# Weight sums by accumulating transfers in DRAM, and one first-layer quadruple on both pairs of K blocks

## The chip, the cores and the metric

The kernel runs on one core of one Trainium2 chip. The metric is device time of one execution in microseconds. The core's engines are TensorE (PE in the profile, with its weight loads as PEld), VectorE (DVE), ScalarE (ACT), GpSimd (POOL) and SyncE (SP, which here only issues DMAs). A difference of about 0.2% is what a measurement of this kernel can tell from none.

## The reference, cut to what matters

```python
q, k, v = x @ wqkv                     # x: 2048 x 640, 32 heads of 20
idx = pos[:, None] - 2 * arange(8)     # each position sees 8 keys, 2 apart
attn = softmax(where(idx >= 0, (q . k[idx]) * scale, -1e9))
a = (attn . v[idx]) @ wo               # 640 x 640
h = x @ w1 + b1                        # 640 x 1728
b = (h * tanh(softplus(h))) @ w2       # Mish, 1728 x 640
g = sigmoid((x * gate_w).sum(-1))
out = g * a + (1 - g) * b              # all in float32
```

## The kernel before, in words

**Precision.** Every float32 operand of a matmul is split into two parts of the fast type fp32r: ACT copies the tile (high part, L466), then POOL or DVE subtracts the high part from the tile (low part, L469). A block product is then three matmuls (high x high, high x low, low x high; `mm3`, L534 to L536), on 128 x 128 weights and 512 or 496 columns.

**Seven products for eight.** Most of the work is written as 2 x 2 blocks and done by the Strassen-Winograd scheme: seven block products in place of eight, on sums of the operands. For activations these sums are the forms t1 to t4; for weights they are s1 to s4. A sum is made once and then split like any other operand.

**Stages.** Tokens are cut into four blocks of 512 (tb), two in each half P. In half 0 and then half 1: projection units u.0 to u.7 (a unit is 8 heads of one half, eight slots of 15 matmuls; units 2 and 3 are done by a pair scheme, `Two`), and quadruples q.P.0 to q.P.5 of the first layer (hidden blocks q and 7 + q, both token blocks of the half, five K blocks: 20 block products if done plainly). Attention of the eight units runs on DVE beside it, from unit to unit, far into the next stage. Then the second layer (`mlp2`, L1414) for all tokens, as products a, b, c, e, g, d, f over seven K steps, and last the output projection `wo_part` (L1580) for each half.

**The quadruple.** Class `Quad` (L1142) applies the seven products to both pairs of K blocks (0, 1 with 2, 3) and does the fifth K block plainly: 18 block products. Class `Single` (L1823) applies them to one pair only: 19. `Plain` takes 20. Its steps are `first`, `second`, `m1` to `m4`, `l1`, `l2`; between them ACT copies a bank of PSUM into the next as its seed (`seed`, L1171). `KIND` (L256) names the class for each quadruple of half 1; half 0 always uses `Quad`. `Quad` needs the forms of x for K pairs 0 and 1, `Single` those of pair 0 only (`x_forms`, L1056).

**Weight sums of the first layer.** `pieces` (L1077) loads a quadruple's weight blocks and makes s1 to s4 by additions on POOL or DVE (`combined`, L1040 to L1046, seen as L1044), in half 0 on 256 columns at a time and in half 1, for `Single`, on 128 columns (four additions for each quadruple). Half 1 makes them again from the weights.

**Weight sums of the second layer and of wo.** `sums_of` (L1251) is called nine times (the word `sum` in the order): it loads two blocks of weights, makes three sums and one more of a narrow part on POOL or DVE (L1266, L1279), a negated copy on ACT (L1285), and stores five pieces in DRAM. Later `load_pair` or `load_two` load and split them. `load_minus` and `load_minus_two` load weights with their sign turned, by ACT and DVE.

**What sets the order.** `Plan` (L69) is a list scheduler that runs while the kernel is built: every operation is a task with an engine, a modelled duration, a rank, the tasks it waits for and the buffers it takes from rings (24 pairs, 8 raw tiles, 8 hidden tiles). `ORDER` (L260) is a text that lists the steps of the first stages; a task's place in it breaks ties of rank. A task marked ANY goes to POOL, or to DVE when it is due within 8 us of TensorE's need (`NEAR`). `BANKS` (L259) says which of two groups of three PSUM banks a step uses. DMAs on SP are issued in the order of the plan; transfers that add to their destination (`accum_op`) are issued by POOL, in order with its other work (L955, L1554).

Of the kernel before, what the change touches and what calls it, by code (L numbers as in the profile page):

```python
# [8 lines left out]
F32 = mybir.dt.float32  # L9
# [268 lines left out]
def kernel(ctx: ExitStack, tc: tile.TileContext, x, wq, wo, w1, b1, w2, out):  # L278
# [125 lines left out]
    s_d = [dram.tile([128, 1280], F32, name=f"s{kc}") for kc in range(KH)]  # L404
# [382 lines left out]
    class Two:  # L787
# [16 lines left out]

        def load_first(self):
            n, w = self.n, self.w
            for i in self.pairs:
                (ra, da), (rb, db), (rc, dc), (rd, dd) = [self.raw(self.hq + h, k, n) for h, k in ((0, i), (1, i), (1, 2 + i), (0, 2 + i))]
# [322 lines left out]
    def last_pieces(P):  # L1131
# [7 lines left out]
        if P:  # L1139
            W1["second"] = ws  # L1140
# [864 lines left out]
```

## Time and profile before

| what | value |
|---|---|
| three timed runs | 613.5, 613.86, 613.88 us (median 613.86) |
| the profiled execution's own time | 614.11 us |
| its span, first to last instruction | 612.3 us |
| granted TensorE clock | 1.000 |
| DMA | 147.01 MB, mean 240 GB/s |

Durations in the prediction come from the profiled execution, whose time stands 1.81 us above its span and 0.25 us above the median of the timed runs. In a row of instructions in order of time the first number is the start in microseconds, the second the duration; then come engine, line, operation, the tile written and the tile read with their shapes, how many instructions are merged in the row, and in brackets the idle time before it and what ended that. A row of a group gives its count, total busy time, mean duration in nanoseconds, and the engine's idle time before it. A row of a stretch gives the busy time of PE, PEld, DVE, ACT and POOL, the granted clock, the DMA engines' busy share and GB/s. A queue's row gives its packets, MB and the time its packets took, as a share of 16 engines' span. A row of transfers gives their count, size and the median time from issue to landing.

### The profile page before, as it was taken

The numbers are of one execution on the slowest core, as the hardware profiler recorded it, in microseconds if no ns is written. First come the engines' busy times: TensorE is split into PE (matmuls) and PEld (weight loads), VectorE is DVE, ScalarE is ACT, GpSimd is POOL, SyncE is SP. The second block draws the span as 40 slices with busy tenths as digits, with TensorE's granted clock in tenths as the row PEclk, the third lists the DMA queues.
The fourth block names the chain that finished last, engine by engine and source line by source line (L and its number), as shares of the span: only waits on it lengthen the run. The fifth ranks groups of instructions, "written<-read, shape, count | busy, mean of one in ns | idle before, by whom it ended". The sixth has DMA issues, their size and how long they took to land.

```text
span 612.3 us, 9208 instructions
## 1 busy us (share of the span) xinstructions
PE 608.3 (99%) x2710; PEld 505.7 (83%) x2710; DVE 578.6 (94%) x517; ACT 387.4 (63%) x887; POOL 354.9 (58%) x334
## 2 busy tenths in 40 slices
PE   9999999999999999999999999999999999999997
PEld 7888888888888888888888888888888888888886
DVE  8799998999999999999999999999999999989956
ACT  7678567766897575666656775784966653736520
POOL 1666799978788915464579566686359864001000
PEclk9999999999999999999999999999999999999999
DMA  9764796749788688876888799989798874979913
GB/s 323 227 206 139 239 280 194 269 150 313 278 288 262 188 235 221 257 235 185 225 243 277 226 318 284 346 236 267 232 329 239 231 226 140 279 251 303 279 65 120
DMA packets 101346, 147.01 MB, mean 240 GB/s; under 512 B 11616, under 2 KB 54624, under 8 KB 101072
## 3 DMA queue, kind: packets, MB, share of 16 engines
q1 hardware_dynamic: 97936, 140.66, 71.1%
q0 software_dynamic: 3072, 5.51, 6.4%
q8 instruction: 21, 0.34, 0.3%
q14 instruction: 29, 0.24, 0.1%
q10 hardware_dynamic: 288, 0.26, 0.1%
HBM read 92.38 MB, written 53.03 MB: 237 GB/s over the span
## 4 chain that ended last, share of the span: by engine, by line
PE 97%; ACT 1%; DVE 1%; issue 0%; POOL 0%
PE qb L534 16%; PE qb L535 16%; PE qb L536 16%; PE sb L535 16%; PE sb L536 16%; PE sb L534 16%; PE qb L698 1%; DVE raw L1044 1%; ACT pair L466 1%; PE sb L442 1%; PE sb L540 0%; PE qb L541 0%; PE sb L541 0%; PE qb L540 0%; POOL raw L1044 0%
## 5 line engine op out<-in xcount | busy, mean ns | idle before, releaser
L469 POOL TENSOR_TENSOR pair<-raw,pair 128x512 fp32r<-128x512 f32 (+3 forms) x136 | 169.5, 1269 | 69.0 <-ACT pair L466 46.9
L466 ACT ACTIVATE pair<-raw 128x512 fp32r<-128x512 f32 (+3 forms) x235 | 137.1, 611 | 53.9 <-DMA raw<-actt 12.6
L536 PE MATMUL sb<-pair,pair 128*128 128x512 f32 (+1 forms) x396 | 153.0, 386 | 0.0
L534 PE MATMUL sb<-pair,pair 128*128 128x512 f32 (+1 forms) x396 | 153.0, 386 | 0.0
L535 PE MATMUL sb<-pair,pair 128*128 128x512 f32 (+1 forms) x396 | 153.0, 386 | 0.0
L534 PE MATMUL qb<-pair,pair 128*128 128x512 f32 (+1 forms) x377 | 145.6, 386 | 0.0
L535 PE MATMUL qb<-pair,pair 128*128 128x512 f32 (+1 forms) x377 | 145.5, 386 | 0.0
L536 PE MATMUL qb<-pair,pair 128*128 128x512 f32 (+1 forms) x377 | 145.4, 386 | 0.0
L591 DVE TENSOR_TENSOR pr<-kvq,qg 128x2560 f32<-128x2560 f32 x32 | 89.8, 2807 | 3.3 <-ACT qg L597 2.3
L637 DVE TENSOR_TENSOR pr<-kvq,pg 128x2560 f32<-128x2560 f32 x32 | 90.2, 2820 | 1.0
L594 DVE TENSOR_REDUCE lg<-pr 128x128 f32<-128x2560 f32 x32 | 90.2, 2818 | 0.7
L641 DVE TENSOR_REDUCE kvq<-pr 128x320 f32<-128x2560 f32 x32 | 90.0, 2814 | 0.4
L534 PEld LDWEIGHTS sb<-pair,pair 128*128 128x128 f32 x396 | 74.3, 188 | 14.9
L535 PEld LDWEIGHTS sb<-pair,pair 128*128 128x128 f32 x396 | 74.3, 188 | 14.8
L536 PEld LDWEIGHTS sb<-pair,pair 128*128 128x128 f32 x396 | 74.3, 188 | 14.7
L534 PEld LDWEIGHTS qb<-pair,pair 128*128 128x128 f32 x377 | 70.8, 188 | 14.4 <-ACT qb L1171 0.5
L536 PEld LDWEIGHTS qb<-pair,pair 128*128 128x128 f32 x377 | 70.8, 188 | 13.8
L535 PEld LDWEIGHTS qb<-pair,pair 128*128 128x128 f32 x377 | 70.8, 188 | 13.7
L469 DVE TENSOR_TENSOR pair<-raw,pair 128x512 fp32r<-128x512 f32 (+3 forms) x99 | 68.6, 714 | 3.7 <-ACT pair L466 3.5
L1044 POOL TENSOR_TENSOR hb<-hb,hb 128x512 f32<-128x512 f32 x42 | 55.0, 1327 | 11.7 <-ACT hb L1177 4.8
L1044 POOL TENSOR_TENSOR raw<-raw,raw 128x128 f32<-128x128 f32 (+3 forms) x49 | 40.5, 840 | 12.9 <-DMA raw<-in_wq 2.9
L469 POOL TENSOR_TENSOR pair<-hb,pair 128x512 fp32r<-128x512 f32 (+2 forms) x29 | 34.9, 1210 | 15.7 <-DMA act<-hb 5.8
(173 smaller groups left out, 755.1 us busy)
## 6 DMA issues: line engine op xcount, KB each, us to landing
actt<-hb SPq DMA_DIRECT2D x52, 256.0 KB, 4.0
raw<-in_w SPq DMA_DIRECT2D x40, 256.0 KB, 4.0
act<-hb SPq DMA_DIRECT2D x38, 256.0 KB, 4.2
raw<-actt SPq DMA_DIRECT2D x37, 256.0 KB, 2.6
raw<-in_wq SPq DMA_DIRECT2D x36, 248.0 KB, 4.0
raw<-act SPq DMA_DIRECT2D x29, 256.0 KB, 4.4
raw<-in_x SPq DMA_DIRECT2D x27, 256.0 KB, 4.0
o<-ot SPq DMA_DIRECT2D x64, 80.0 KB, 3.2
```

Source lines behind the costliest of these rows:

```text
L442: nc.tensor.matmul(warm_banks[i % 3].t[:, :n], ones[:, :128], ones[:, :n], start=i < WARM, stop=True, skip_group_check=True)
L466: a = add("ACT", act_ns(n), lambda: A.activation(hi(), raw(), AF.Copy), after, rank=rank, take=take, hold=hold)
L469: return (V if e == "DVE" else G).tensor_tensor(lo(), raw(), hi().bitcast(F32), op=OP.subtract)
L534: nc.tensor.matmul(ps, ah, bh, start=first, stop=False, skip_group_check=more)
L535: nc.tensor.matmul(ps, ah, bl, start=False, stop=False, skip_group_check=more)
L536: nc.tensor.matmul(ps, al, bh, start=False, stop=last, skip_group_check=more)
L591: return V.tensor_tensor(pr, window(kv, s0, 0), qg[:, :, None, :].to_broadcast([128, 2, W, QF]), op=OP.mult)
L594: V.tensor_reduce(lg_w[:, s0:s0 + 2], pr.rearrange("p s w (h d) -> p s w h d", d=DH), op=OP.add, axis=AX.X)
L637: V.tensor_tensor(pairs.rearrange("p s k i (h d) -> p s k i h d", d=DH), vw, pg[:, s0:s0 + 2].rearrange("p s (k i) h -> p s k i h", i=2)[: ...
L641: V.tensor_reduce(q[:, s0:s0 + 2], pairs.rearrange("p s k i f -> p s f k i"), op=OP.add, axis=AX.XY)
L698: nc.tensor.matmul(ps.t[:, :n], X[0, kc].t[:, a, i * 128:(i + 1) * 128], WQ[0, kc].t[:, b, :n], start=a == b and kc == 0, stop=False)
L1044: return (V if e == "DVE" else G).tensor_tensor(t.t[:, i:i + n], a.t[:, j:j + n], b.t[:, k:k + n], op=op)
```

## The change

1. `KIND` becomes `SSSSSF`: quadruple 5 of half 1 is done by `Quad`, with the forms of the second K pair made for half 1 as well (`forms.1.1` in the order).
2. The first layer's sums made in half 0 are stored in DRAM (`kept_sums`), and half 1 loads them in place of making them again. (The same is written into `Two` for unit 6, which is not in `PAIRS`, so that code issues nothing.)
3. `sums_of` no longer computes on an engine: each of four sums for w2, and four for wo, is one copy from DRAM to DRAM on SP and one accumulating transfer issued by POOL. Those for w2 are let go one at a time after step `l2` of quadruples 0 to 3 of half 1, those for wo after products a, b, c and e of the second layer. Weights are laid out on the host so that each sum is one wide block (seven blocks side by side).
4. The accumulating transfers add. So the signs of the sums change: forms of the hidden activations are subtracted the other way round (a3, a4), and the evacuations of c, g, d and f and their like in `wo_part` swap add and subtract. Product d of the second layer reads its PSUM bank on DVE directly, without the copy by ACT. The second set of wo's last weights, with the sign turned, is no longer needed.
5. `ORDER` and `BANKS` are written anew throughout; the word `sum` still stands in the order, but nothing is done for it.

```diff
-KIND = 'SSSSSS'
+KIND = 'SSSSSF'
...
-u.0.5 u.0.4 u.0.7 u.0.6 q.0.0.first wq.1 q.0.0.m1 q.0.0.second sum q.0.0.m3 last.0 q.0.0.m4 u.1.0 u.1.2 pieces.0.1 pieces.0.2 q.0.0.l1 q.0.1.first
+u.0.5 u.0.6 q.0.0.first pieces.0.1 u.0.4 u.0.7 q.0.0.second q.0.0.m1 q.0.1.first wq.1 q.0.0.m2 pieces.0.2 q.0.0.m3 q.0.0.m4 q.0.1.second u.1.0
...
-q.1.3.m3 q.1.2.l1 q.1.4.m1 u.7.6 q.1.3.l1 sum q.1.3.l2 q.1.4.second q.1.4.m4 pieces.1.5 q.1.4.m2 lastw.1 u.7.0 q.1.4.m3 q.1.5.first q.1.4.l2 q.1.5.m1
-q.1.5.second q.1.4.l1 q.1.5.m4 q.1.5.m3 rest.2 q.1.5.m2 q.1.5.l2 q.1.5.l1 last.2 last.3 rest.3
+q.1.4.m1 q.1.3.m2 q.1.4.second q.1.5.first q.1.4.m4 q.1.4.m3 q.1.3.l2 q.1.5.second q.1.4.l2 q.1.5.m2 rest.1 q.1.5.m1 q.1.4.m2 q.1.5.m3 q.1.4.l1
+q.1.5.m4 sum q.1.5.l1 u.7.6 q.1.5.l2 u.7.7 u.7.4 u.7.3 u.7.2 last.2 u.7.5 last.3 u.7.1 u.7.0 rest.2 rest.3
...
-        if P:
+        if P and KIND[q] == "S":
             ra, rb, rc = [raw_buf() for _ in range(3)]
...
-            dc = dma(lambda: rc.t[:, 256:384], lambda: w1[b][:, 0], take=[rc], size=65536)
-            s1 = combined(128, (rc, 384), (rc, 256), (rb, 128), OP.add, [db, dc], rank=SOON)
-            s3 = combined(128, (rc, 256), (ra, 0), (rc, 256), OP.subtract, [da, s1], rank=SOON)
-            s2 = combined(128, (rc, 0), (rc, 384), (ra, 0), OP.subtract, [da, s1], rank=SOON)
-            s4 = combined(128, (rc, 128), (ra, 256), (rc, 0), OP.subtract, [s2], rank=SOON)
+            dc = dma(lambda: rc.t, lambda: w1s_d[q, 0], kept_sums[q], take=[rc])
...
+        if P:
+            d4 = add("SP", 1350, four, take=[r4], size=262144)
+            do, db = [dma(lambda r=r: r.t, lambda i=i: w1s_d[q, i], kept_sums[q], take=[r]) for i, r in ((0, o1), (1, rb))]
...
+        if not P:
+            if KIND[q] == "F":
+                kept_sums[q] = [dma(lambda i=i, r=r: w1s_d[q, i], lambda r=r: r.t, w, rank=1.0, hold=[r]) for i, r, w in ((0, o1, [s4]), (1, rb, [s3]))]
...
+    def let_go(P, q, t):
+        if P and q < 4:
+            sums_of(w2, KH, s_d, "s", 1 + q, t)
...
+    def sums_of(w, k, to, key, n, at):
+
+        a1, a1r, a2 = k * 256, k * 384, k * 640
+        first = {1: lambda: w[0][:, a1r:a2], 2: lambda: w[0][:, :a1r], 3: lambda: w[0][:, :a1r], 4: lambda: w[1][:, :a1r]}[n]
+        more, wide = {1: (lambda: w[1][:, a1r:a2], a1), 2: (lambda: to[1], a1), 3: (lambda: w[0][:, a1r:a2], a1), 4: (lambda: to[2], a1r)}[n]
+        c = dma(lambda: to[n], first, [at], rank=0.5, size=512 * (a1 if n == 1 else a1r))
+        before = done[key, n // 2] if n % 2 == 0 else []
+        done[key, n] = [add("POOL", 900, lambda: G.dma_start(out=to[n][:, :wide], in_=more(), accum_op=OP.add, max_dma_last_dim=2048), [c] + before,
+                            rank=-0.5, size=1024 * wide, late=1500)]
...
-                        z = stage(True)
-                        read["v", P, j] = c = copy(z, bank["v", P, j], [ends["d", "v", P, j]], [z])
                         b = zw[key]
-                        v = two("ANY", b, b, z, OP.add, [c, b.done])
-                        y[key].used = v = two("ANY", b, y[key], b, OP.subtract, [v, y[key].done])
+                        read["v", P, j] = v = two("DVE", b, bank["v", P, j], b, OP.subtract, [ends["d", "v", P, j], b.done])
+                        y[key].used = v = two("ANY", b, y[key], b, OP.add, [v, y[key].done])
...
+                if k < 4:
+                    sums_of(wo, 2, so_d, "so", 1 + k, last)
...
-                quads[key] = ({"S": Single, "P": Plain}[KIND[n[1]]] if n[0] else Quad)(*key)
+                quads[key] = ({"S": Single, "P": Plain, "F": Quad}[KIND[n[1]]] if n[0] else Quad)(*key)
```

More of the change, by code (lines that the diff above doesn't have):

```diff
@@ L1300, in load_minus_two @@
-    def load_minus_two(srcs):
-        raw, p = stage(True), pair_buf()
-        def both():
-            for i, s in enumerate(srcs):
-                nc.sync.dma_start(raw.t[:, i * 256:(i + 1) * 256], s())
-        d = add("SP", 900, both, take=[raw], size=262144)
-        a = add("ACT", act_ns(512), lambda: A.activation(p.t[:, 0], raw.t, AF.Copy, scale=-1.0), [d], rank=SOON, take=[p], hold=[raw])
-        b = add("DVE", dve_ns(512), lambda: V.scalar_tensor_tensor(p.t[:, 1], raw.t, -1.0, p.t[:, 0].bitcast(F32),
-                op0=OP.mult, op1=OP.subtract), [a], rank=SOON, hold=[raw, p])
-        p.ready = [a, b]
-        return p
@@ new lines, in load_parts, with parts @@
+    def load_parts(srcs, after=(), minus=False, wide=True):
+        raw, p, n = stage(wide), pair_buf(), sum(m for m, _ in srcs)
+        def parts():
+            at = 0
+            for m, src in srcs:
+                nc.sync.dma_start(raw.t[:, at:at + m], src())
+                at += m
+        d = add("SP", 450 * len(srcs), parts, after, take=[raw], size=n * 512)
+        if minus:
+            a = add("ACT", act_ns(n), lambda: A.activation(p.t[:, 0, :n], raw.t[:, :n], AF.Copy, scale=-1.0), [d], rank=SOON, take=[p], hold=[raw])
+            b = add("DVE", dve_ns(n), lambda: V.scalar_tensor_tensor(p.t[:, 1, :n], raw.t[:, :n], -1.0, p.t[:, 0, :n].bitcast(F32),
+                    op0=OP.mult, op1=OP.subtract), [a], rank=SOON, hold=[raw, p])
+            p.ready = [a, b]
+        else:
+            p.ready = split(lambda: raw.t[:, :n], lambda: p.t[:, 0, :n], lambda: p.t[:, 1, :n], n, [d], "ANY", [raw], [p], SOON)
+        return p
@@ L1327, with block, load_stack @@
+    def block(of, k, i):
+        return [(256, lambda: of()[:, i * 256:(i + 1) * 256]), (128, lambda: of()[:, k * 256 + i * 128:k * 256 + (i + 1) * 128])]
     HALF = "bgf"
-    def load_stack(src, n, minus=False, after=()):
-        raw, p = stage(True), pair_buf()
+    def load_stack(srcs, minus=False, after=()):
+        raw, p, n = stage(True), pair_buf(), sum(m for m, _ in srcs)
         def twice():
             for i in range(2):
-                nc.sync.dma_start(raw.t[i * FR:(i + 1) * FR, :n], src())
-        d = add("SP", 900, twice, after, take=[raw], size=n * 512)
+                at = 0
+                for m, src in srcs:
+                    nc.sync.dma_start(raw.t[i * FR:(i + 1) * FR, at:at + m], src()[:FR])
+                    at += m
+        d = add("SP", 900 * len(srcs), twice, after, take=[raw], size=n * 512)
@@ L1459, in after_product @@
                         z = y[key] = zp[key]
-                        z.done = two("DVE", z, z, bank["u", P, j], OP.add, [ends["c", "u", P, j], z.done])
+                        z.done = two("DVE", z, bank["u", P, j], z, OP.subtract, [ends["c", "u", P, j], z.done])
                     elif name == "e":
@@ L1475, in after_product @@
                         b = y[key]
-                        result(b, 2 * P, 2 + j, [two("DVE", b, b, bank["v", P, j], OP.subtract, [ends["f", "v", P, j], b.used])])
+                        result(b, 2 * P, 2 + j, [two("DVE", b, b, bank["v", P, j], OP.add, [ends["f", "v", P, j], b.used])])
                 if name in "bd":
@@ L1732, in wo_part @@
         for j in range(2):
-            y[j].done = two("DVE", y[j], y[j], bank[f"u{j}"], OP.add, [ends[f"u{j}"], y[j].done])
+            y[j].done = two("DVE", y[j], bank[f"u{j}"], y[j], OP.subtract, [ends[f"u{j}"], y[j].done])
         for j in range(2):
```

203 lines of the change are left out of this document (90 added, 113 removed).

## The prediction

> **What bounds the kernel now.** I read the page first, then the matmuls in order of time, then the busy time by stretch, the groups by shape, and the DMA queues. The page:
>
> ```profile
> span 612.3 us, 9208 instructions
> PE 608.3 (99%) x2710; PEld 505.7 (83%) x2710; DVE 578.6 (94%) x517; ACT 387.4 (63%) x887; POOL 354.9 (58%) x334
> PE 97%; ACT 1%; DVE 1%; issue 0%; POOL 0%
> ```
>
> TensorE is busy 608.3 of 612.3 us and holds 97% of the chain that ended last. Matmuls overlap, though, so a busy PE may still hide stalls; they show only in the step from one start to the next. Ten consecutive matmuls of a first-layer quadruple (first and last of the ten), and nine of a projection (first and last of the nine):
>
> ```profile
> 63.83 0.39 PE L536 MATMUL sb<-kvq,pair 128*128 128x512 f32 x1
> ...
> 65.87 0.39 PE L536 MATMUL sb<-kvq,pair 128*128 128x512 f32 x1
> ```
> ```profile
> 74.12 0.38 PE L534 MATMUL qb<-pair,pair 128*128 128x496 f32 x1
> ...
> 75.88 0.38 PE L536 MATMUL qb<-pair,pair 128*128 128x496 f32 x1
> ```
>
> (65.87 − 63.83) / 9 = 0.227 us is the step of a 512-column matmul; (75.88 − 74.12) / 8 = 0.220 us that of a 496-column one. Against these two steps I went through all 2710 starts. Beyond the first 7 us only three places stand out, and these are their rows:
>
> ```profile
> 32.62 0.39 PE L534 MATMUL qb<-kvq,pair 128*128 128x512 f32 x1
> 33.98 0.39 PE L534 MATMUL sb<-pair,pair 128*128 128x512 f32 x1
> 34.37 0.64 ACT L466 ACTIVATE pair<-raw 128x496 fp32r<-128x496 f32 x1
> 34.88 0.61 ACT L1171 ACTIVATE qb<-qb 128x512 f32<-128x512 f32 x1
> 35.11 0.39 PE L536 MATMUL sb<-pair,pair 128*128 128x512 f32 x1
> 35.55 0.50 PE L534 MATMUL qb<-pair,pair 128*128 128x512 f32 x1
> 35.89 0.40 PE L535 MATMUL qb<-pair,pair 128*128 128x512 f32 x1
> ```
> ```profile
> 76.01 0.18 ACT L708 ACTIVATE hx<-qb 128x16 f32<-128x16 f32 x1
> 76.24 0.50 PE L534 MATMUL qb<-kvq,pair 128*128 128x512 f32 x1
> 76.58 0.39 PE L535 MATMUL qb<-kvq,pair 128*128 128x512 f32 x1
> ```
> ```profile
> 146.97 0.39 PE L536 MATMUL qb<-pair,pair 128*128 128x512 f32 x1
> 147.33 0.50 PE L534 MATMUL qb<-kvq,pair 128*128 128x512 f32 x1
> 147.67 0.40 PE L535 MATMUL qb<-kvq,pair 128*128 128x512 f32 x1
> ```
>
> At 35 us: (35.55 − 35.11 − 0.227) + (35.89 − 35.55 − 0.227) = 0.33 us. At 76 us: (76.24 − 75.88 − 0.220) + (0.34 − 0.227) = 0.25 us. At 147 us: (0.36 − 0.227) + (0.34 − 0.227) = 0.25 us. Together 0.83 us: that is all that better feeding of TensorE can return. So the time is the number of matmuls times their step, and a change pays by taking matmuls away, or costs by a new stall.
>
> **The change, part by part.** *Matmuls.* A quadruple is 20 block products of three matmuls. Seven products on one pair of K blocks (Single) take 19, on both pairs (Quad) 18. The letter F moves quadruple 5 of the second half from 19 to 18: 3 x 0.227 = **0.68 us off the path**. Nothing else changes a count: the second layer's and the output projection's products are the same list with signs moved.
>
> *The stall at 35 us.* Today `first` of quadruple 0 (32.62) is followed at once by `second` (33.98) and `m1` (35.55). `m1` writes a bank that ACT seeds from `first`'s bank, and that seed (34.88) stood behind a split (34.37). The new order puts `first` ahead of u.0.4 and u.0.7, 30 matmuls or 6.8 us earlier against `m1`, so the seed has long run. Next late would be the forms that `second` and `m1` read; they were in time at 33.98 and 35.55, and the new place of these two is the same within 0.2 us. I take **0.33 us off**. The other two stalls fall on a matmul that opens a qb bank; at 76 us ACT had just emptied one (76.01). Banks and order are written anew everywhere, so such meetings are dealt again: I keep their **0.50 us**; the bounds are 0 and, upward, the rivals.
>
> *Work taken from and given to POOL, DVE and ACT.* By shape:
>
> ```profile
> L1279 POOL TENSOR_TENSOR raw<-raw,raw 128x512 f32<-128x512 f32 x9 | 12.0, 1330 | 1.3 <-DMA raw<-in_wo 1.0
> L1266 POOL TENSOR_TENSOR raw<-raw,raw 128x256 f32<-128x256 f32 x9 | 7.3, 806 | 3.2 <-DVE zt L925 1.5 <-DVE hb L1044 1.4
> L1266 POOL TENSOR_TENSOR raw<-raw 128x256 f32<-128x256 f32 x9 | 6.7, 742 | 17.5 <-DVE hb L1189 10.0 <-DVE pair L469 2.8 <-DMA raw<-in_wq 2.6
> L1266 POOL TENSOR_TENSOR raw<-raw 128x128 f32<-128x128 f32 x9 | 4.8, 529 | 2.5 <-DVE pg L627 1.4 <-DVE zt L925 0.9 <-DVE pr L591 0.2
> L1044 POOL TENSOR_TENSOR raw<-raw,raw 128x128 f32<-128x128 f32 x19 | 8.8, 476 | 6.3 <-DMA actt<-hb 2.3 <-DVE hb L1044 1.6 <-DVE ot L547 1.3
> L1044 DVE TENSOR_TENSOR raw<-raw,raw 128x128 f32<-128x128 f32 x5 | 2.0, 406 | 0.0
> L1044 POOL TENSOR_TENSOR raw<-raw,raw 128x512 f32<-128x512 f32 x7 | 10.3, 1476 | 2.0 <-DVE raw L1044 2.0
> L469 POOL TENSOR_TENSOR pair<-raw,pair 128x512 fp32r<-128x512 f32 x90 | 117.2, 1319 | 41.0 <-ACT pair L466 27.6 <-DVE hb L1189 3.6 <-issue 3.3
> L1554 POOL DMA_DIRECT2D ot<-ot x8 | 7.1, 884 | 12.1 <-DMA ot<-o 6.7 <-DMA ot<-ot 5.4
> ```
>
> Out go the nine weight sums (12.0 + 7.3 + 6.7 + 4.8 = 30.8 us) and the second half's 24 small sums (8.8 + 2.0 = 10.8 us). In come four forms of x (4 x 1.48), five more splits (5 x 1.32) and eight accumulating issues (8 x 0.88): 19.6 us. Net 22 us less on POOL, all of it beside a TensorE that does not wait for it: worth nothing beyond the stalls above. It is also cover for what the change adds.
>
> *Signs.* Moved between add and subtract, operations in the second layer's and wo's evacuations keep their size. In product d the ACT copy that freed a bank goes, and a DVE read frees it instead:
>
> ```profile
> 521.59 0.60 ACT L1429 ACTIVATE hb<-qb 128x512 f32<-128x512 f32 x1 [2.60 <-PE qb L536]
> L591 DVE TENSOR_TENSOR pr<-kvq,qg 128x2560 f32<-128x2560 f32 x32 | 89.8, 2807 | 3.3 <-ACT qg L597 2.3
> ```
>
> The read may stand behind an attention operation of 2.81 us. Five groups of six matmuls (5 x 6 x 0.227 = 6.8 us) lie between the end of d on a bank and f's start on it: hidden, and at most 2.81 us more than today if that cover were gone.
>
> *Transfers.* Second-layer sums: four copies DRAM to DRAM (1792 or 2688 columns of 128 rows: 0.92 + 3 x 1.38 = 5.05 MB) and four accumulations (3 x 0.92 + 1.38 = 4.13 MB). By the order's product counts they are let go between about 232 and 326 us. Nobody needs them before product c, some 110 us after the last is let go, so their own duration is free. What they take is DMA time.
>
> ```profile
> q1 hardware_dynamic: 97936, 140.66, 71.1%
> q0 software_dynamic: 3072, 5.51, 6.4%
> ```
> ```profile
> 232.00:345.00 113.00, 113.00 (x509) 95.17 (x508) 111.22 (x76) 69.42 (x174) 71.86 (x79) 1.00 0.83 242
> 378.00:400.00 22.00, 22.00 (x99) 18.22 (x98) 21.83 (x17) 14.87 (x32) 13.19 (x13) 1.00 1.00 324
> ```
>
> Plain transfers cost 0.711 x 612.3 / 140.66 = 3.1 us of all 16 engines per MB, accumulating ones 0.064 x 612.3 / 5.51 = 7.1 us. So 5.05 x 3.1 + 4.13 x 7.1 = 45 us come into that stretch. Five of the old sums leave it (640 KB loaded and 640 KB stored each, 6.55 MB, 20 us), and kept sums and more forms add some 2 MB (6 us). Busy share: (0.83 x 113 + 31) / 113 = 1.10, more than there is. By bytes: 242 + (5.05 + 4.13 − 6.55 + 2) / 113 us = 283 GB/s, below the 324 GB/s that moved at 378 to 400 us with TensorE full. Shares add up concurrent packets; bytes are nearer to what the queues must deliver, so I take **no PE time**, and keep the other end as a rival. The Trainium skill, DMA: Bandwidth & Descriptors, section Bandwidth, measures 341 GB/s for 1 MB against 138 for 64 KB; by that the new 9.18 MB would be about 27 us (an estimate from the page), the share 0.95, and the rival weaker. No transfer of that size is in this trace.
>
> *Waits added.* An accumulation waits on POOL for its copy to land; behind it in order stand POOL's splits, and behind those TensorE. The row for such a wait:
>
> ```profile
> 280.24 0.83 POOL L955 DMA_DIRECT2D actt<-actt  x1 [6.26 <-DMA act<-hb]
> ```
> ```profile
> 270.00:290.00 20.00, 20.00 (x92) 16.93 (x91) 19.80 (x13) 12.11 (x32) 10.27 (x14) 1.00 0.70 201
> ```
>
> POOL stood 6.26 us there, and no matmul in that stretch was late: 6.26 us of cover. The largest copy is 1.38 x 3.1 = 4.3 us: hidden, unless the queue ahead of it is full. On SP the copies wait for `l2`'s last matmul and the kept sums for their stores, which are a whole half older; neither holds a load long.
>
> *Sum.* −0.68 − 0.33 = −1.01 us. Span 612.3 → 611.3; the profiled execution was 614.11 (1.81 around the span) → 613.10; it stood 0.25 above the median of 613.86, so the median goes to **612.85**, 0.16% less.
>
> **The rivals.** *All stalls go (faster).* If 76 and 147 us are dealt well too, −0.68 − 0.83 = −1.51: 612.35 (612.6 with one of them). For it: ACT is 63% busy and gets no heavier. Against: they are chance meetings, and every stretch gets a new order.
>
> *The accumulations crowd out the loads (slower).* Place: 232 to 345 us. An accumulation of 0.92 MB is 6.5 us of all engines, that of 1.38 MB 9.8 us. Loads and POOL work held that long exceed the 6.26 us of cover by 3 x 0.24 + 3.54 = 4.3 us: 617.1. It decides as soon as a load is more than 6.3 us late. For: the share of 1.10. Against: 324 GB/s at share 1.00 with TensorE full, and the median load, which would have to take two and a half times as long:
>
> ```profile
> raw<-in_w SPq DMA_DIRECT2D x40, 256.0 KB, 4.0
> ```
>
> The Trainium skill, same page, section Queues, rings and completion order, says that a DMA engine takes its queues in turn, packet by packet. By that a load beside an accumulation takes twice its time, 4.0 us more, which is under 6.26, and the rival's 4.3 us would not come.
>
> *A late start (no change).* Pieces of quadruple 1 are asked for some microseconds earlier, when the DMA engines are full:
>
> ```profile
> 5.00:10.00 5.00, 5.00 (x23) 4.09 (x22) 4.59 (x8) 4.26 (x7) 0.00 (x0) 1.00 1.03 374
> ```
>
> One load late by half its 4.0 us gives back 2.0: 614.85. Against: two weight sums' loads leave the first 70 us.
>
> **How the numbers follow.** Forecast 0.45 (both stalls kept, or up to two more of 0.25: 612.65 to 613.35), one or both gone 0.32, late start 0.08, crowding 0.15. This kernel's runs tell about 0.2% (1.23 us) from no change: faster is below 612.63, slower above 615.09. Faster 0.32, same 0.45 + 0.08 = 0.53, slower 0.15. Range: from 612.35 less the runs' 0.36 downward spread, 612.0, to the late start and its spread, 615.1; left out are 0.15 and little more.
>
> **What would show it.** Right: 2707 matmuls; no wide step at `m1` of quadruple 0; no L1266 or L1279 on POOL; eight larger accumulations on q0, DMA share up in 232 to 345 us with starts still 0.227 apart. Wrong: wide steps clustered behind the accumulations (crowding), or in the first 50 us (late start), or a sum of wide steps beyond 7 us well away from 0.50.

## The result, and the profile after

| kernel | median of the timed runs | lowest to highest | profiled execution, span |
|---|---|---|---|
| before | 613.68 us | 613.33 to 613.88 | 614.11, 612.3 us |
| changed | 622.41 us | 621.67 to 622.96 | 622.96, 621.2 us |

The ratio is 1.0142, with a 95% interval of 1.0125 to 1.0160: the change makes the kernel 1.4% slower. The forecast was 612.85 us, and the range ended at 615.1.

The page of the changed kernel, the lines that answer to the first three of the prediction:

```profile
span 621.2 us, 9068 instructions
PE 610.0 (98%) x2707; PEld 505.3 (81%) x2707; DVE 585.9 (94%) x526; ACT 389.8 (63%) x882; POOL 321.7 (52%) x281
```

There are 2707 matmuls, three fewer, as forecast. The span is 8.9 us longer all the same, so there must be some 9.6 us of new waits. The waits of TensorE name them (in total, times, longest):

```profile
PE sb L537 <- ACT qb L1216: 1.8, 1, 1.8
PE qb L543 <- ACT pair L469: 1.7, 1, 1.7
PE sb L543 <- DVE pair L1345: 1.2, 1, 1.2
PE qb L544 <- POOL pair L472: 0.9, 1, 0.9
PE sb L445 <- PEq L1982: 0.8, 1, 0.8
PE sb L544 <- POOL pair L472: 0.6, 1, 0.6
```

(Lines of helpers stand three higher than before: the three matmuls of a product are L537 to L539, the low part of a split is L472. L543 and L544 are the two matmuls of the last, 64-row K step.) The 0.8 us on PEq is the start of the program and was there before. The other five make two places. I took every start of the 2707 against the step of 0.227 or 0.220 us, as the prediction did. Beyond the first 7 us the steps are wider by about 10.5 us in all, against 0.83 before; the difference is the 9.6 us:

- **At 428 to 441 us, 6.86 us**, the end of product b in the second layer. Its TensorE rows in order of time (start, duration):

```profile
428.80 0.39 PE L539 MATMUL sb<-pair,pair 128*128 128x512 f32 x1
430.41 0.47 PE L543 MATMUL sb<-pair,pair 128*128 128x512 f32 x1 [1.23 <-DVE pair L1345]
431.45 0.50 PE L544 MATMUL sb<-pair,pair 128*128 128x512 f32 x1 [0.57 <-POOL pair L472]
...
434.54 0.39 PE L539 MATMUL qb<-pair,pair 128*128 128x512 f32 x1
436.59 0.51 PE L543 MATMUL qb<-pair,pair 128*128 128x512 f32 x1 [1.66 <-ACT pair L469]
437.94 0.79 PE L544 MATMUL qb<-pair,pair 128*128 128x512 f32 x1 [0.85 <-POOL pair L472]
438.54 0.63 PE L537 MATMUL qb<-pair,pair 128*128 128x512 f32 x1
```

Four waits, and behind the last of them seven wide steps, one of 0.59 and six of 0.41 to 0.43 us, about half rate: the granted clock from 437.9 to 441.1 us is 0.51. These seven make 1.5 of the 6.86 us.

- **At 47.6 us, 2.04 us**: a matmul waits 1.77 us for the ACT copy that seeds its bank (L1216), and the step after it is 0.11 us late.
- At 59.1, 463.6 and 43 us, 0.6, 0.7 and 0.2 us. These three were not examined by themselves.

From 150 to 400 us, where the four large accumulations run, no matmul is over 0.1 us late. The three stalls of before (35, 76, 147 us) are gone.

**What is late at 428 us.** The last K step of product b needs the 64-row rest block of the first layer's second half. That block goes over a long chain: VectorE turns it, SyncE stores it in eight pieces (h<-kvq) and loads it back in two (kvq<-h), ScalarE does Mish (L967 before, L997 after), then come a store, a load and a split. SyncE's own rows of the changed kernel, and the two operations of Mish before and after:

```profile
409.41 0.33 SPq L502 DMA_DIRECT2D h<-kvq  x1
...
411.72 0.85 SPq L1312 DMA_DIRECT2D raw<-in_w  x2
...
415.62 1.31 SPq L502 DMA_DIRECT2D h<-kvq  x2
419.46 0.92 SPq L1312 DMA_DIRECT2D raw<-in_w  x2
...
422.61 0.42 SPq L502 DMA_DIRECT2D h<-kvq  x1
```
```profile
411.71 0.72 ACT L967 ACTIVATE kvq<-kvq,bias 64x512 f32<-64x512 f32 x1
416.65 0.71 ACT L967 ACTIVATE kvq<-kvq,bias 64x512 f32<-64x512 f32 x1
```
```profile
426.46 0.73 ACT L997 ACTIVATE kvq<-kvq,bias 64x512 f32<-64x512 f32 x1
...
433.64 1.28 ACT L997 ACT_TABLE_LOAD   x1
434.94 0.72 ACT L997 ACTIVATE kvq<-kvq,bias 64x512 f32<-64x512 f32 x1
...
435.92 0.61 ACT L469 ACTIVATE pair<-raw 128x512 fp32r<-128x512 f32 x1
```

Before, all eight stores were issued between 402.1 and 406.0 us; now they take from 409.4 to 423.0, and Mish of the second block ends 18 us later. VectorE is not what makes them late: it turned both blocks by 399.2 us (397.2 before). The TensorE rows above wait for this chain in two ways. At 430.41 and 431.45 us they wait for weights and a load that SyncE issued only at 423.1 to 426.1 us, behind the stores. At 436.59 and 437.94 us they wait for the split of the first block's values (435.92). The load that it reads landed at 433.90 us, but the split stood on ScalarE behind the second block's Mish and the table load ahead of that.

**What SyncE waits for.** SyncE does not work more in this stretch: from 384 to 424 us it issues 55 transfers and is busy 26.9 us, before 58 and 26.4 us. What changed is what it waits for. Of its waits at 336 to 409 us, 19.7 us are for the landing of an earlier transfer; before it is 5.3 us, and most of the waits were for POOL and ACT. The longest rows (in total, times, longest), changed and then before:

```profile
SPq L502 <- DMA raw<-act: 9.4, 7, 3.2
```
```profile
SPq L499 <- POOL pair L469: 5.7, 11, 1.2
SPq L499 <- ACT hb L1177: 5.3, 4, 3.4
```

The semaphores in the trace tell why. SyncE's transfers report their landing on eight semaphores in turn, and in every run of this case no issue starts sooner than 0.015 us after the transfer of eight issues before has landed (663 pairs in the changed kernel). For example, SyncE stands still from 416.9 to 419.46 us; the transfer of eight issues before, the one of 411.72, landed at 419.44. So at most eight of its transfers are under way: one that lands late holds up the row, and a block that takes two transfers takes two of the eight places. No run changed the number of semaphores, so this is read from the traces; the experiments below change what fills the places.

### The profile page after: what moved, and what is told of

The parts are those of the page before. It is cut to its first block, busy times and chain, and to the rows that moved or that the text cites. A ratio compares the mean times of both kernels' runs of the same rounds, so it can differ in the third digit from the quotient of the medians.

```text
span 621.2 us, 9068 instructions
## 1 busy us (share of the span) xinstructions
PE 610.0 (98%) x2707; PEld 505.3 (81%) x2707; DVE 585.9 (94%) x526; ACT 389.8 (63%) x882; POOL 321.7 (52%) x281
## 3 DMA queue, kind: packets, MB, share of 16 engines
q1 hardware_dynamic: 92336, 139.35, 68.9%
q0 software_dynamic: 5984, 10.82, 11.7%
## 5 line engine op out<-in xcount | busy, mean ns | idle before, releaser
L472 POOL TENSOR_TENSOR pair<-raw,pair 128x512 fp32r<-128x512 f32 (+4 forms) x137 | 172.5, 1280 | 106.2 <-ACT pair L469 34.8
L469 ACT ACTIVATE pair<-raw 128x512 fp32r<-128x512 f32 (+3 forms) x235 | 135.5, 610 | 47.9 <-DMA h<-kvq 7.6
L537 PE MATMUL qb<-pair,pair 128*128 128x512 f32 (+1 forms) x389 | 150.7, 388 | 0.0
L539 PE MATMUL qb<-pair,pair 128*128 128x512 f32 (+1 forms) x389 | 150.5, 387 | 0.0
L538 PE MATMUL qb<-pair,pair 128*128 128x512 f32 (+1 forms) x389 | 150.5, 387 | 0.0
L537 PE MATMUL sb<-pair,pair 128*128 128x512 f32 (+1 forms) x383 | 148.1, 387 | 2.2 <-ACT qb L1216 1.8
L539 PE MATMUL sb<-pair,pair 128*128 128x512 f32 (+1 forms) x383 | 148.0, 386 | 0.0
L538 PE MATMUL sb<-pair,pair 128*128 128x512 f32 (+1 forms) x383 | 147.9, 386 | 0.0
L537 PEld LDWEIGHTS sb<-pair,pair 128*128 128x128 f32 x383 | 71.9, 188 | 17.2 <-ACT qb L1216 2.2
L537 PEld LDWEIGHTS qb<-pair,pair 128*128 128x128 f32 x389 | 73.3, 189 | 14.6 <-ACT sb L1216 0.2
L538 PEld LDWEIGHTS qb<-pair,pair 128*128 128x128 f32 x389 | 73.3, 188 | 14.5
L539 PEld LDWEIGHTS qb<-pair,pair 128*128 128x128 f32 x389 | 73.2, 188 | 14.4
L539 PEld LDWEIGHTS sb<-pair,pair 128*128 128x128 f32 x383 | 71.9, 188 | 14.3 <-POOL pair L472 0.3
L538 PEld LDWEIGHTS sb<-pair,pair 128*128 128x128 f32 x383 | 71.9, 188 | 14.2
L472 DVE TENSOR_TENSOR pair<-raw,pair 128x512 fp32r<-128x512 f32 (+2 forms) x98 | 71.1, 749 | 2.7 <-ACT pair L469 2.5
L469 ACT ACTIVATE pair<-hb 128x512 fp32r<-128x512 f32 (+3 forms) x63 | 37.4, 594 | 24.6 <-DMA hb<-actt 8.1
L1074 POOL TENSOR_TENSOR raw<-raw,raw 128x256 f32<-128x256 f32 (+2 forms) x31 | 32.9, 1071 | 18.5 <-DVE raw L1074 15.1
```

Source lines behind the costliest of these rows:

```text
L469: a = add("ACT", act_ns(n), lambda: A.activation(hi(), raw(), AF.Copy), after, rank=rank, take=take, hold=hold)
L472: return (V if e == "DVE" else G).tensor_tensor(lo(), raw(), hi().bitcast(F32), op=OP.subtract)
L537: nc.tensor.matmul(ps, ah, bh, start=first, stop=False, skip_group_check=more)
L538: nc.tensor.matmul(ps, ah, bl, start=False, stop=False, skip_group_check=more)
L539: nc.tensor.matmul(ps, al, bh, start=False, stop=last, skip_group_check=more)
L1074: return (V if e == "DVE" else G).tensor_tensor(t.t[:, i:i + n], a.t[:, j:j + n], b.t[:, k:k + n], op=op)
```

## The experiments

Theories at the start: (1) SyncE is too full, since each weight block now takes two transfers; (2) the new order; (3) the transfers of the sums.

### The order and the code, exchanged

e1 is the changed code with the `ORDER` and `BANKS` of before (`forms.1.1` put in ahead of `pieces.1.5`); e2 is the code of before with the changed order and banks (without `forms.1.1`, `KIND` SSSSSS).

> The changed kernel's code, F included, under the order and banks of the kernel before (the forms of the second K pair put in where quadruple 5 needs them). Theory 1 (the weight blocks of products a and b now take two SP issues each, so the narrow hidden columns' stores come too late on SP and product b's last step waits for them): the double issues are still there, 617 to 621 us with wide steps near 428 to 441 us. Theory 2 (the new order is the cause, in the start and at b's end): 612.3 to 613.7 us. Theory 3 (copies and accumulations crowd the queues): 619 to 622 us.

> The code of the kernel before, all Single in half 1, under the new order and banks (without the forms of the second K pair). Theory 1: no double issues, so b's end is clean and only the stalls of the start stay, 614.5 to 617 us. Theory 2: everything stays, 622 to 623.5 us (0.68 us of matmuls more). Theory 3: no accumulations, 613 to 615 us.

e1 took 649.97 us (1.0589 [1.0572, 1.0606]), e2 653.36 (1.0644 [1.0628, 1.0660]). Both are some 40 us slower than before, with waits all over: in e1 up to 7.0 us at 455 us, in e2 up to 4.5 us at 227 us. So order and code are fitted to each other, and an exchange tells nothing of either. Neither theory was borne out; the method was wrong.

### Two edits that let the scheduler deal anew

e3 raises the rank of the rest block's stores in half 1. e4 leaves out the eight copies and eight accumulations; products c, e, g and d load unsummed weights in their place.

```diff
 e3: -        d = turned_out(lambda: h_d[tb], blocks, [t], [b], late)
     +        d = turned_out(lambda: h_d[tb], blocks, [t], [b], late, -0.5 if P else 1.0)
 e4: -    s_d = {n: dram.tile(...) for n in (1, 2, 3, 4)}
     +    s_d = {n: w2[0] for n in (1, 2, 3, 4)}        # so_d likewise; sums_of does nothing
```

> The changed kernel with one edit: the eight stores of half 1's narrow hidden columns get a rank of -0.5 in place of 1.0, so that SP issues them ahead of the second layer's loads. SP's order is the same up to there. Theory 1: the 6.9 us at b's end go, 622.4 - 6.9 = 615.5 us (615 to 616.5), the start's 2.8 us stay. Theory 2 (unit 7 last makes the chain late before these stores): 619 to 622.4 us. Theory 3: 620 to 622.4 us.

> The changed kernel without its eight copies and eight accumulations; products c, e, g and d load unsummed weights of the same size in their place, so this leaves the weight sums out. Theory 1: 621 to 622.4 us, little gained. Theory 2: 621 to 622.4 us. Theory 3: 613.5 to 616 us, the wide steps at 428 to 441 us gone.

e3 took 623.86 us (1.0154 [1.0116, 1.0193]): Mish of the second block began 11 us earlier (423.77 us), but the weights of the same K step, issued behind it at 422.4 us, came late: ScalarE stood 5.24 us for them, with the splits of that step queued behind, and TensorE 5.2 us. e4 took 623.51 us (1.0158 [1.0141, 1.0175]): the stall at 428 us was gone, and 3.8 us of new ones stood at 341 to 347 us, more at 445 and 452. A changed task changes the places of hundreds of others, so a stall that goes and one that comes can't be set against each other. From here on every edit kept the plan (its modelled durations and sizes) as it was, and changed only what is issued for a task, so that each remaining instruction kept its place.

### With the order held: issues, accumulations, halos

e5 narrows all eight accumulations to 64 columns. e6 fetches a block of 384 columns by one transfer of neighbouring columns, and so leaves out 128 of the block's own. e7 cuts unit 7's halo copies to 16 partitions. e12 narrows only the four accumulations of the second layer.

```diff
 e5: -G.dma_start(out=to[n][:, :wide], in_=more(), ...
     +G.dma_start(out=to[n][:, :64], in_=more()[:, :64], ...
 e6:  def parts():
     +    if len(srcs) == 2 and n == 384:
     +        nc.sync.dma_start(raw.t[:, :n], srcs[0][1](n))      # 384 neighbours
     +        return
 e7: +end = lambda b: 16 if u == 7 and b == 112 else b            # rows of the halo copy
 e12: as e5, for key "s" only
```

> The changed kernel, but each of the 8 accumulations adds only its first 64 columns (so the sums are wrong in the other columns); the copies and every instruction's place stay. The bytes accumulated fall from 4.13 MB to 0.26 MB. Theory A (SyncE's longer row of issues and the transfers already under way make the chain behind the last K step of product b late; the sums' bytes have no part in it): the stalls at 428 to 441 us stay near 6.9 us and the one at 47.6 us stays near 1.9 us, time 621.5 to 623. Rival B (the accumulations crowd out the transfers of that chain, that of out's weights at 422 us above all): the stalls at 428 to 441 us fall below 3 us, time 617 to 619.5.

> The changed kernel, but each block of 384 weight columns is fetched by one SyncE transfer of 384 neighbouring columns in place of two of 256 and 128 (so other columns than the product needs); all else, each instruction's place too, stays. SyncE has 34 issues fewer, about 0.3 to 0.5 us each, most of them in 300 to 430 us. Theory A (SyncE's issues): the stores of the rest at 409.4 to 422.6 us come 3 to 6 us earlier, the stalls at 428 to 441 us fall from 6.9 to under 2.5 us, time 617 to 619. Rival C (not issues but the time transfers take to land sets the chain): stalls stay over 5 us, time 621 to 622.5. The stall at 47.6 us stays near 1.9 us by both.

> The changed kernel, but unit 7's halo copies, issued at 373 to 382 us, move 16 partitions' rows instead of all (so part of that unit reads old rows); each instruction's place stays. Rival C (bytes under way at 373 to 392 us make SyncE's queue and the landings late): the halos land in 2 to 3 us instead of 5.6 and 8.2, the stalls at 428 to 441 us fall from 6.9 to under 4 us, time 618 to 620. Theory A (issues): they fall by under 1 us, time 621 to 622.5. The stall at 47.6 us stays.

> The changed kernel, but only the four accumulations of the second layer's weights (issued at 234, 282, 297 and 336 us) add just their first 64 columns, so that those sums are wrong elsewhere; out's own four accumulations stay whole, and every instruction keeps its place. With all eight narrow, the stall at 428 to 441 us fell from 6.9 to 3.8 us. Theory B1 (the last big one, under way from 336 to some 355 us, holds back the fetches of that stretch, and SyncE's row carries the delay to 409 us): the stall is 3.5 to 4.5 us again, time 619 to 620. Rival B2 (out's accumulation at 422 us, in the midst of the late chain, is what counts): the stall stays over 6 us, time 621.5 to 623.

| kernel | time, us (ratio to before) | SyncE's waits for landings, 336 to 409 us | first store of the rest | second Mish | excess steps, 400 to 450 us |
|---|---|---|---|---|---|
| before | 613.7 | 5.3 | 402.14 | 416.65 | none |
| changed | 622.41 (1.0142) | 19.7 | 409.41 | 434.94 | 6.9 |
| e5, accumulations narrow | 619.39 (1.0085 [1.007, 1.010]) | 8.0 | 407.96 | 432.42 | 3.8 |
| e12, those of w2 narrow | 619.65 (1.0097 [1.0080, 1.0114]) | 8.4 | 408.03 | 431.86 | 2.5 |
| e6, one issue a block | 616.04 (1.0043 [1.0025, 1.0060]) | 4.9 | 402.62 | 426.86 | none |
| e7, small halos | 617.95 (1.0065 [1.0036, 1.0095]) | 17.8 | 405.12 | 430.78 | 0.7 |

Each of these cuts takes a good part of the stall or all of it; the chain is late by a sum, and TensorE feels only what exceeds the cover.

*The issues.* e6 takes out 34 SyncE transfers (and no bytes): the first store comes 6.8 us earlier, Mish ends 8.1 us earlier, and no step is over 0.1 us late after 100 us. These are SyncE's rows of e6 in the same view as above:

```profile
402.62 0.32 SPq L502 DMA_DIRECT2D h<-kvq  x1
...
405.77 0.38 SPq L1311 DMA_DIRECT2D raw<-in_w  x1
...
409.41 0.43 SPq L1311 DMA_DIRECT2D raw<-in_w  x1
...
413.89 0.32 SPq L502 DMA_DIRECT2D h<-kvq  x1
```

A block costs SyncE 0.38 or 0.43 us in one transfer (L1311) where it cost 0.85 or 0.92 in two (L1312). Theory A's number (617 to 619) was even a little too high. But its reason, the time of the issues, does not carry the gain: only eleven of the 34 stand before the first store at 409 us, some 5 us of issues, and two more before 428 us (I had expected most of them there). With them go places on the row, and SyncE's waits for landings fall from 19.7 to 4.9 us. The rows of memory that a packet moves are longer too (1.5 KB in place of 1 KB and 512 B), which no run separates from the count; the time of all packets on SyncE's queue falls only from 428 to 422 us (68.9% of 621.2 and 68.7% of 614.4).

*The accumulations.* The last large one is issued at 335.8 us. Stretches of the changed kernel and of e12, and rows of their transfers at 336 to 344 us (count, size, median time to landing):

```profile
340.00:350.00 10.00, 10.00 (x46) 8.45 (x46) 9.79 (x9) 9.28 (x21) 1.72 (x2) 1.00 1.06 241
```
```profile
340.00:350.00 10.00, 10.00 (x47) 8.45 (x46) 9.79 (x10) 9.65 (x22) 1.71 (x2) 1.00 0.46 156
```
```profile
s<-s POOLq DMA_DIRECT2D x1, 1344.0 KB, 16.8
raw<-act SPq DMA_DIRECT2D x4, 256.0 KB, 11.4
```
```profile
raw<-act SPq DMA_DIRECT2D x4, 256.0 KB, 3.5
...
s<-s POOLq DMA_DIRECT2D x1, 32.0 KB, 5.2
```

With the whole accumulation, which lands after 16.8 us, the DMA engines' share is 1.06 where it is 0.46 with the narrow one, and a load of activations lands in 11.4 us where it takes 3.5 without it (the row's median knows two of the four; by the semaphores the four take 10.1 to 12.5 us, and 3.5 to 5.1 in e12). TensorE stays full in both rows (10.00 of 10.00). The loads' delay reaches it 80 us later, over SyncE and the rest block's chain. Both kernels issue the same 671 SyncE transfers in the same order, so the path can be followed. Measured against TensorE's place, SyncE is 2.9 us ahead in e12 at 347 us and 2.0 us ahead at the first store of the rest; only at 384 us is the lead gone for a moment, and why it comes back was not found out. Behind an earlier accumulation it is 3.1 us ahead at 295 us too, but level again at 319. Theory B1 said 619 to 620 and 3.5 to 4.5 us; the time was 619.65, the stall 2.5 us, with 1.3 us of smaller steps behind it at 455 to 461 us. So the four of w2 carry what all eight do (e5), and the one at 422 us does not count. That of the four it is the last is read from SyncE's row, not from a run of its own. In e5 I had held theory A against this rival; the rival was half right.

*The halos.* e7 gave 617.95 us with runs from 615.5 to 620.8, so its size is less certain. Fewer bytes under way at 373 to 392 us help the same chain: SyncE's row stays within about 1 us of the changed kernel's until 384 us and is 5.7 us ahead at the first store. Rival C foresaw the gain and theory A did not, though the halos land in 4.4 and 6.5 us and not in 2 to 3. The halos are not part of the change; they are there before as well.

### The stall at 47.6 us

The matmul waits for a ScalarE copy, that for another one, and that for a VectorE operation which began late. VectorE's rows just before, in the changed kernel, then GpSimd's row beside them, then VectorE's in the kernel before:

```profile
43.43 1.20 DVE L955 TENSOR_SCALAR zt<-zt 128x8 f32<-128x8 f32 x1
44.66 0.20 DVE L956 RECIPROCAL gate<-zt 128x8 f32<-128x8 f32 x1
44.89 0.94 DVE L957 TENSOR_SCALAR gc<-gate 128x8 f32<-128x8 f32 x1
...
46.00 2.78 DVE L594 TENSOR_TENSOR pr<-kvq,qg 128x2560 f32<-128x2560 f32 x1
```
```profile
40.83 4.97 POOL L472 TENSOR_TENSOR pair<-raw,pair 128x512 fp32r<-128x512 f32 x4 [0.82 <-DVE pr L594]
```
```profile
44.23 0.17 DVE L925 TENSOR_SCALAR zt<-zt 128x8 f32<-128x8 f32 x1
44.44 0.20 DVE L926 RECIPROCAL gate<-zt 128x8 f32<-128x8 f32 x1
44.67 0.21 DVE L927 TENSOR_SCALAR gc<-gate 128x8 f32<-128x8 f32 x1
```

Two operations on eight numbers a partition take 1.20 and 0.94 us where they took 0.17 and 0.21. Each ends just when a GpSimd split does: the first at 44.62, the third split at 44.59; the second at 45.83, the fourth split at 45.80 (40.83 + 4.97). The reciprocal between them, beside the same fourth split, is not slowed. e8 puts reciprocals in the place of both, which leaves the gates' own arithmetic out:

```diff
-            V.tensor_scalar(zt[:, P], zt[:, P], 1e30, 1.0, op0=OP.min, op1=OP.add)
+            V.reciprocal(zt[:, P], zt[:, P])
-            V.tensor_scalar(gc[:, :8], gate[:, P], -1.0, 1.0, op0=OP.mult, op1=OP.add)
+            V.reciprocal(gc[:, :8], gate[:, P])
```

> The changed kernel, but in the gates' four small VectorE operations the two TENSOR_SCALAR (1.20 and 0.94 us in the changed kernel's trace beside a busy GpSimd, 0.17 and 0.21 us in the kernel before) are reciprocals like their neighbour (0.20 us), so that the gates' values are wrong; each instruction's place stays. Theory D (the two wait for GpSimd's operation under way, on a port that both engines use; with one input and outside the doubled rate a VectorE operation does not): they take 0.2 us each, VectorE is free 1.7 us earlier, the stall at 47.6 us falls from 1.9 to under 0.5 us, time 620.5 to 621. Rival E (any small VectorE operation there is slow, or the stall's cause is ScalarE's own queue): both stay near 1 us, or the stall stays over 1.5 us, time 622 to 622.5.

The time was 618.89 us (1.0086 [1.0066, 1.0106]), and VectorE's rows of e8, beside the same four splits of GpSimd, are:

```profile
43.74 0.20 DVE L955 RECIPROCAL zt<-zt 128x8 f32<-128x8 f32 x1
43.97 0.20 DVE L956 RECIPROCAL gate<-zt 128x8 f32<-128x8 f32 x1
44.21 0.20 DVE L957 RECIPROCAL gc<-gate 128x8 f32<-128x8 f32 x1
```

At the place of the stall, now 48.0 us, 0.31 us is left of 2.04. The gain of 3.5 us is more than this stall's 2.0. The spans of the two profiled executions differ by 1.9 us (621.2 and 619.3); 1.4 us of that lie in the first 50 us, and the stall at 428 us is no smaller (7.2 us). So I take the rest of the 3.5 for the spread of the runs (618.12 to 621.10), and the size from e10 below. The Trainium skill, SBUF — State Buffer, section Who interferes with whom, says that VectorE in a two-port mode, which TENSOR_SCALAR can enter, shares a port pair with GpSimd, and that the later one is blocked until the other's instruction ends. The rows agree, down to both ends; the mode itself is in no row.

### A version without both causes, and the kernel before with the issues

e9 keeps all the work, and lays the weights out in DRAM so that each block's 256 and 128 columns are neighbours (one transfer; 38 issues fewer by the trace; two of four accumulations then run in 1 KB pieces). e10 adds to that layout the gates as two sigmoids on ScalarE, in place of an exponential there and three VectorE operations. e11 is the kernel before with its blocks fetched in two transfers.

```diff
 e9: -(256, lambda: of()[:, i * 256:(i + 1) * 256]), (128, lambda: of()[:, k * 256 + i * 128:...])
     +(384, lambda: of()[:, i * 384:(i + 1) * 384])
 e10:+A.activation(gate[:, P], zt[:, P], AF.Sigmoid)
     +A.activation(gc[:, :8], zt[:, P], AF.Sigmoid, scale=-1.0)    # for the three DVE operations
 e11:+if tuple(a.shape) == (128, 384):
     +    nc.sync.dma_start(a[:, :256], b[:, :256])
     +    a, b = a[:, 256:], b[:, 256:]
```

> The changed kernel with all of its work, but the weights lie in DRAM so that each block of 384 columns is one row of neighbours (256 and 128 columns side by side, the 256 others behind them): 40 SyncE issues fewer; two of the four accumulations of each weight then run in pieces of 1 KB, and every instruction's place stays. Theory A (SyncE's issues carry the stall at 428 to 441 us): that stall is gone as in the run with one issue a block, the one at 47.6 us (1.9 us) stays, time 615.5 to 617. Rival C (that run was quick because it read other columns, or accumulations in short pieces cost what the issues gave): over 618.

> The layout of the run above, and the gates as two sigmoids on ScalarE in place of an exponential there and three VectorE operations (two of them the TENSOR_SCALAR that stood 1.20 and 0.94 us beside GpSimd); all work is done, every other instruction's place stays. Theory A with D (the two causes are apart and add up): no stall over 0.7 us after the first 7 us, time 613.0 to 614.0, within 0.2% of the kernel before, since three matmuls fewer are worth 0.68 us and small stalls of about 1 us are left. Rival E (one stall only hands its time to the next place): over 615.

> The kernel before, but each weight block of 384 columns is fetched by two SyncE transfers of 256 and 128 columns, as the changed kernel does: 34 issues more, every instruction's place stays. Theory A1 (issues are dear only where the order leaves SyncE no room, and the kernel before has room): 613.4 to 614.5. Rival A2 (34 more issues of 0.3 to 0.5 us make any order late): a stall of 3 us or more in 400 to 445 us, time 617 to 620.

e9 took 616.16 us (1.0036 [1.0022, 1.0050]), e10 613.84 (0.9997 [0.9989, 1.0006]), e11 613.90 (1.0004 [0.9994, 1.0013]). TensorE's waits in e9 and in e10, down to 0.2 us:

```profile
PE sb L537 <- ACT qb L1216: 1.7, 1, 1.7
PE sb L445 <- PEq L1987: 0.8, 1, 0.8
PE sb L539 <- POOL pair L472: 0.5, 1, 0.5
PE qb L537 <- ACT hx L711: 0.3, 1, 0.3
```
```profile
PE sb L445 <- PEq L1988: 0.8, 1, 0.8
PE sb L539 <- POOL pair L472: 0.2, 1, 0.2
```

The two causes are apart and add up: 622.41 − 616.16 = 6.25 us for the layout with fewer issues (6.86 us of excess steps are gone), 616.16 − 613.84 = 2.32 us for the gates. By the steps, 1.8 us of the gates' gain lie at 48 us, where the two small operations were. Another 0.5 us lie at 59 us, a stall that e8 keeps; so that part comes from another piece of e10's edit. With both mended, the changed kernel is as fast as the one before. And e11 shows that the 34 issues cost nothing where there is room: before's SyncE takes them without one late step more (TensorE's excess beyond 7 us is the same three stalls), and its waits for landings at 336 to 409 us stay at 4.4 us. It is the issues together with the changed order and its accumulations that cost 6.25 us.

## Why the prediction was wrong

- *Three matmuls fewer, −0.68 us*: right. 2707 matmuls, and in e10, where the waits are gone, the last one starts at 608.36 us, against 608.91 before. The whole of the forecast gain is not seen even there: it asked for 0.9984 of before's time, and e10 has 0.9997 [0.9989, 1.0006].
- *The stall at 35 us goes*: right, and so do those at 76 and 147 us, of which I kept 0.50 us. "Dealt again" was right, and too small: the changed kernel has 1.5 us of small waits (at 43, 59.1 and 463.6 us), e10 about 1.06 us beyond 7 us, as against 0.83 before. In e10 −0.68 + 0.23 = −0.45 us lies near the −0.55 us measured at the last matmul (profiled executions, so within their spread).
- *GpSimd 22 us lighter, worth nothing*: its busy time fell by 33 us (354.9 to 321.7), and no row shows a gain from it. But I counted only its amount. What mattered was which of its work lay beside VectorE at 43 to 46 us, and that cost 2.0 us. Step "worth nothing beyond the stalls above" failed there. My rival of a late start had the place (the first 50 us) and the size (2.0 us) by luck: its cause, a late load, was another.
- *Transfers, no PE time*: failed, and this is the larger step. I weighed the accumulations against the matmuls of their own stretch, 232 to 345 us. There the forecast holds: not one late matmul, a DMA share of 0.93 (I had 1.10) and 251 GB/s (283). But loads landed in 10.1 to 12.5 us where e12 has 3.5 to 5.1, SyncE waited for landings and came later, and the delay reached TensorE at 428 us. My rival "the accumulations crowd out the loads" had the mechanism in part: its sign, a load more than 6.3 us late, came true for three of the four, and its price of 4.3 us is of the right size (e12 gives 2.8 us back, 622.41 − 619.65), but its place was wrong. The cover of 6.26 us that I named was that of one GpSimd wait at 280 us; the chain at 428 us had its own, unexamined. The sentence on the Trainium skill's rule, that queues are served in turn and a load beside an accumulation takes twice its time, was too mild: these four take 2.0 to 3.3 times.
- *Issues on SyncE*: missing from the sum. I counted what leaves and what comes by bytes and by GpSimd's instructions. My "neither holds a load long" looked at two waits of SyncE and not at its row. That every weight block of the second layer is fetched in two transfers instead of one stands in the diff (`block` returns two pieces), and I never priced it. The time of the issues would not have been the price: eleven before the first store, at some 0.45 us each, on a row that is busy two thirds of the time before and after. What counts is that only eight transfers are under way, and that the accumulation keeps them there longer: 19.7 us of waits for landings against 5.3. Taking the issues out gave 6.25 us back (e9), taking w2's accumulations out 2.8 (e12), and the kernel before takes the same issues for nothing (e11). So none of them has a price by itself.
- *Of the signs that would show it wrong*, "in the first 50 us" and "a sum of wide steps well away from 0.50" came true; "clustered behind the accumulations" did too, 90 us behind.

Why the changed order leaves the rest block's chain so little room was not found out; it is a property of a whole schedule, and e1 to e4 show that a single edit does not isolate it. Nor was quadruple 5 tried by itself; its worth is the count of matmuls alone.

## What to carry to other kernels

Price a change on every engine's queue, the DMA-issuing one too: count its issues and how many may be under way at once, look at what its waits are for, and follow a delay down to the longest chain that runs over that queue, since a full TensorE beside the transfer says nothing about the stall 80 us on. When order and durations are fitted to each other by a scheduler, test a suspicion with edits that keep every instruction in its place; an edit that lets the schedule move tells little. And look for small operations that take several times what they took before: what runs on the engine beside them may be their price.

## What the runs showed of the hardware

- An accumulating DRAM to DRAM transfer of 1344 KB took 16.8 us to land; over the whole changed run these transfers cost 2.2 times as much engine time per MB as plain ones (the queues' rows below: 0.117 x 621.2 / 10.82 = 6.7 us, 0.689 x 621.2 / 139.35 = 3.1 us).

```profile
q1 hardware_dynamic: 92336, 139.35, 68.9%
q0 software_dynamic: 5984, 10.82, 11.7%
```

- Most SyncE issues of the changed kernel take 0.32 to 0.5 us. At 384 us four of them span 3.96 us; the first takes 1.60 us, and 1.04 us of the rest is a wait until 386.78 us, when the transfer of eight issues before had landed (386.76).
- Beside the accumulation of 1344 KB, four loads of 256 KB landed after 10.1 to 12.5 us; with 32 KB accumulated, after 3.5 to 5.1 us.
- Waits of TensorE of 1.66 and 0.85 us close together (0.86 and 0.84 in e5) were followed by some seven steps at about 0.43 us in place of 0.227, 1.4 to 1.5 us more, at a granted clock of 0.51 and 0.50. Other pairs were not: 1.23 and 0.57 us at 430 us, and 0.3 and 0.8 in e12 (granted clock 1.00 behind them). Nor was the single wait of 1.77 us at 47.6 us. What decides it is not shown.
